# Splitting the last 256 tokens into two units of 128 and regrouping the opening in a two-layer transformer kernel

## The chip, the cores and the metric

The kernel runs on one NeuronCore of one Trainium2 chip. The metric is the device time of one execution in microseconds (us). Six runs of the kernel before gave a median of 1552.33 us, from 1551.97 to 1553.21.

The core has five engines with separate instruction streams, each executed in order. The text calls them PE (matrix multiply), ACT (activation functions), DVE (vector), POOL (GpSimd) and SP (here it only issues DMAs). PE writes its results into PSUM, eight banks of 128 partitions x 512 fp32.

## The reference: what is computed

2048 tokens of width 512 pass through attention, MLP, attention, MLP. Both attention layers share one set of weights, and so do both MLPs.

```python
def _A_ref(x, wqkv, wo):                       # D = 512, H = 32 heads of 16
    qkv = (x @ wqkv).reshape(B, S, 3, H, Dh).transpose(2, 0, 3, 1, 4)
    p = softmax(einsum("bhqd,bhkd->bhqk", q, k) * Dh ** -0.5)
    return einsum("bhqk,bhkd->bhqd", p, v).transpose(0, 2, 1, 3).reshape(B, S, D) @ wo
def _B_ref(x, w1, b1, w2, b2):                 # F = 1376
    return gelu(layernorm(x) @ w1 + b1) @ w2 + b2
x = x + _A_ref(layernorm(x), A_wqkv, A_wo)
x = x + _B_ref(layernorm(x), B_w1, B_b1, B_w2, B_b2)
x = x + _A_ref(layernorm(x), A_wqkv, A_wo)
x = x + _B_ref(layernorm(x), B_w1, B_b1, B_w2, B_b2)
```

A head has only 16 channels, so most of the work is not the multiplication but the exponentials: 2 layers x 32 heads x 2048 x 2048 of them.

## The kernel before

**Tiles.** Tokens lie in 16 tiles of 128. Query tokens are handled in units: four units of four tiles in layer 1 (the code's L == 1), and in layer 3 (the second attention) three units of four tiles and two of two tiles, tokens 12-13 and 14-15 (`build_segments`). Heads go in eight groups of four. A segment is one unit and one head group. The first unit of each layer is done in two parts over the keys (layer 1: key tiles 0 to 3 first, then 4 to 15), since its keys aren't all ready.

**A score tile** fills one PSUM bank with 512 columns: a unit of four tiles has 512 query columns for one key tile and one head; a unit of two tiles has two key tiles of 256 columns each, as two matmuls. There are 4096 score tiles in all. The four heads of a group lie in four row groups of PE (32 rows each), so up to four score tiles run side by side (L1470). The products with V (PV, L1658) use four column groups in the same way and accumulate in one bank (`ACCB`, 6).

**Exponentials.** ACT takes score tiles in groups: one instruction (L1455) reads two or three adjacent banks and writes bf16 probabilities. DVE takes about a quarter of the tiles in another way ("D tiles"): it adds a constant to the score, stores 16-bit integers whose bits are a bf16 approximation of the exponential (L1555), and adds shifts to make three more (L1588); each of the four is multiplied with a scaled V and accumulated. So a D tile costs PE four PV turns and an ACT tile one.

**Banks.** A pool "mb" owns banks 0 to 5 and 7. In the opening (layer 1, unit 0, part 0) scores use banks 0 to 3 in groups of two and two (`flow_scores`), and banks 4, 5 and 7 are left for other matmuls. Then `wide` is set: banks 0 to 5 belong to scores, in groups of three and two, and D tiles use bank 5 or 7.

**The opening.** While ACT does the scores of key tiles 0 to 3, the keys and values of tiles 4 to 15 are made (`job_qkv_tile` with "kv"): normalise into `xn` (L891, L893), transpose by a DMA that SP issues into `xnT` (L927), eight matmuls (L950) into a bank of mb, copies by DVE (L956, L973), squares by POOL (L991), norms by DVE (L1015). When the norms of all 16 tiles are there, `job_scl` makes one bound per head (L1157 to L1166), which scales the queries of every later segment (L1196). So part 1 can't begin before the last key tile is done.

**The end of a segment** (`job_segend`): DVE transposes the accumulated bank (L1688), takes a reciprocal (L1714) and writes the scaled output to `ob` (L1723). When eight head groups are done, `job_post` issues four transposing DMAs into `OT` (L1732), multiplies with wo (L1737), adds the residual, normalises, transposes (L1784), and `job_ffn` does w1 (L1792), bias (L1816), GELU on ACT (L1827, L1828, with one table load before and one behind, as exp and GELU lie in different tables), w2 (L1835) and the sum (L1837).

**The end of the kernel** (`job_tail`, `tail_tile`): for tokens 14-15 the residual and the first seven head groups are put into a bank ahead of the last one (L1898, L1737); after the last scores a GELU of one column loads the table (L1869); the last head group is added (L1903), the bank normalised straight from PSUM (L1907 to L1914), transposed by PE (L1916, L1918); then w1, GELU with the bias from PSUM (L1889) and w2 (L1874) follow chunk by chunk, 11 chunks of 128 hidden channels, and the result is copied out (L1879).

**The order of the work** is made at build time. `Sched` holds tasks with priorities and modelled durations, and always places next the one that can start first; its choices become the five in-order streams. `Hint.ORDER` is a string of digits: every four score groups it picks one of ten settings of the planner's thresholds (such as how idle DVE must be to take a D tile). Another string gives another order of the whole program. A last pass (`refill`) fills modelled PE gaps with matmuls on zeros (L1359, L1361, L1363), which keep PE busy and change no result.

Of the kernel before, what the change touches and what calls it, by code (L numbers as in the profile page):

```python
# [506 lines left out]

class Hint:
# [3 lines left out]
    ORDER = '1000505400844554053031008034310130004043277211200001031009349005902383344374250110710071520000700010897013450230200545450055021090000330009921105703053220050405100500340302221091514024010003201130050000322000100000400300044000720830007030033701430000245354444034510580430030403022240093200204095050982000792049091440853'  # L512
# [13 lines left out]
class Builder:  # L526
# [16 lines left out]
    def build_segments(self):  # L543
        self.segs = []
        four = [tuple(range(4 * c, 4 * c + 4)) for c in range(self.NC)]
        self.units = {1: four, 3: four[:3] + [four[3][:2], four[3][2:]]}
# [369 lines left out]
    def job_qkv_tile(self, L, tt, slot, i, left, prio, what):  # L916
# [10 lines left out]
        yield self.dma(lambda e: e.dma_start_transpose(xnT, xnr), [RX], [RXT], prio, 1.31, 1.2)  # L927
# [443 lines left out]
    def flow_scores(self):  # L1371
# [11 lines left out]
        for b in range(4):  # L1383
            S_.retire("mb", b, ("ret", b))
        last = {}
        while True:
# [6 lines left out]
            if not self.wide and not (sg["L"] == 1 and sg["nparts"] == 2 and sg["part"] == 0):  # L1393
                self.wide = True
                gi += gi % 2
                for b in (4, 5):
                    S_.retire("mb", b, ("ret", b))
            if self.wide:
# [49 lines left out]
            if len(ops[0]) > 1:  # L1448
                ops = [[o[i] for o in ops] for i in range(len(ops[0]))]
# [231 lines left out]
    def job_segend(self, sg):  # L1681
# [33 lines left out]
        if L == 3 and qc == len(self.units[3]) - 1 and hg == 7:  # L1715
            ob = self.obl[:, :].rearrange("p (b r) -> p b r", r=32)
            yield Task("dve", 1.2, [I(lambda e: e.tensor_tensor(out=ob[:, :, 0:16], in0=T[:, :, 0:16], in1=rv.unsqueeze(2).broadcast_to([128, nb, 16]), op=ALU.mult), [RA, ("rv", a)], [("obl",)], 0.147 + 0.268 * W / 512)])
# [22 lines left out]
    def post_prio(self, L, qc):  # L1740

        return 0.95 if L == 1 and qc >= self.NC - 2 else 2.2
# [45 lines left out]
    def mm_w1(self, L, qc, fc, b, pr, W, off=0):  # L1788
        M = 128 if fc < self.NFC - 1 else self.FLAST
        yield ("keys", [("w1", L, qc, fc)])  # L1790
        for c0 in (0, 2):
            yield Task("pe", pr if c0 == 0 else min(pr, HINT.LIN2), [I(lambda e, c=c: e.matmul(self.ps[0:M, b, off:off + W], lhsT=self.w1(fc, c), rhs=self.yT[:, c, 0:W], start=(c == 0), stop=(c == 3)),  # L1792
                                    [("wf", fc)] + [("yT", i) for i in range(W // 128)], [("ps", b)], 0.216 * W / 512, [("ps", b)]) for c in (c0, c0 + 1)])

    def gt(self, fc, i, W):
        if fc == self.NFC - 1:
            return self.g10[:, i * 128:(i + 1) * 128]
        return self.gv[:, fc * W + i * 128:fc * W + (i + 1) * 128]
# [220 lines left out]
```

## Time and profile before

| | before |
|---|---|
| median of six runs | 1552.33 us |
| the profiled execution | 1552.41 us, its span 1550.4 us, granted PE clock 1.000 |
| PE, DVE, ACT busy | 97%, 95%, 98% of the span |
| exponentials on ACT | 687 of two tiles, 586 of three |
| first exponential starts, first one behind the opening starts, last one ends | 20.95, 87.10, 1529.56 us |
| matmuls | 16485 |

The span runs from the first to the last instruction; the 2.0 us between it and the time lie around it. "Busy" is the union of an engine's instructions. Matmuls are pipelined, so one of 128 columns is shown with 219 ns though the next starts 56 ns later: start times tell more than durations. In a row of the timeline the first number is the start, the second the length of the merged row; what stands in brackets is idle time of that engine ahead of the row, and what ended it.

### The profile page before, as it was taken

The page shows a single profiled execution, that of the slowest core. Times are in us where ns is not written, and L with a number is a line of the kernel's source. Part 1 is how long each engine was busy: PE and PEld are TensorE (multiplying, and loading weights), DVE is VectorE, ACT ScalarE, POOL GpSimd, SP SyncE. Part 2 cuts the span into 40 slices and gives each one's busy share as a digit, 9 for nine tenths or more (in the row PEclk, how much of TensorE's full clock was granted, in tenths as well). Part 3 has the DMA queues.
Part 4 walks back from the last instruction along what each step waited for, and adds up shares of the span by engine and source line. Part 5 has one row for each costly group of instructions (what it writes and reads, how often), then busy time and mean ns, then how long its engine had stood idle before and what let it go on. Part 6 is the DMA issues. An engine that isn't in the chain of part 4 may idle for free.

```text
span 1550.4 us, 39363 instructions
## 1 busy us (share of the span) xinstructions
PE 1505.2 (97%) x16485; PEld 475.0 (31%) x16485; DVE 1465.3 (95%) x3272; ACT 1512.3 (98%) x1361; POOL 321.7 (21%) x558
## 2 busy tenths in 40 slices
PE   9999999999999999999999999999999999999998
PEld 3222222222222222222222322223222222344444
DVE  8799999999999999999999899999999999999993
ACT  8989999999999999999999999999999999999996
POOL 3585322002220021102312227310001000020100
PEclk9999999999999999999999999999999999999999
DMA  6673012214311222214732232310102000221200
GB/s 163 123 143 99 29 32 40 56 22 89 76 42 51 45 65 70 56 28 95 142 70 60 59 81 69 63 25 22 33 21 42 22 18 23 41 42 36 51 20 22
DMA packets 212450, 88.68 MB, mean 57 GB/s; under 512 B 183307, under 2 KB 207152, under 8 KB 212272
## 3 DMA queue, kind: packets, MB, share of 16 engines
q1 hardware_dynamic: 212272, 86.16, 25.3%
q8 instruction: 129, 2.11, 0.6%
q14 instruction: 49, 0.40, 0.1%
HBM read 34.65 MB, written 19.48 MB: 35 GB/s over the span
## 4 chain that ended last, share of the span: by engine, by line
ACT 47%; DVE 27%; PE 22%; issue 2%; POOL 1%; DMA 0%; SPq 0%; POOLq 0%; DVEq 0%
ACT PT L1455 44%; DVE dp L1555 11%; DVE dp L1588 8%; PE ps L1470 7%; PE ps L1658 5%; ACT h L1827 2%; PE ps L1835 2%; PE ps L1792 2%; PE ps L950 2%; PE ps L1359 1%; DVE accT L1688 1%; DVE n L1015 1%; DVE st L873 1%; PE ps L1068 1%; PE ps L1363 1%
## 5 line engine op out<-in xcount | busy, mean ns | idle before, releaser
L1455 ACT ACTIVATE PT<-ps 128x1536 bf16<-128x1536 f32 (+1 forms) x1273 | 1428.5, 1289 | 18.8 <-PE ps L1470 16.5
L1555 DVE TENSOR_SCALAR dp<-ps 128x512 uint16<-128x512 f32 x964 | 642.1, 681 | 27.3 <-PE ps L1470 25.6
L1470 PE MATMUL ps<-QT,KT 32*128 32x512 bf16 (+1 forms) x4608 | 600.9, 359 | 19.2 <-ACT PT L1455 6.0
L1588 DVE TENSOR_SCALAR dp<-dp 128x1024 uint16<-128x1024 uint16 (+1 forms) x1464 | 567.9, 429 | 3.6 <-PE ps L1658 0.9
L1658 PE MATMUL ps<-PT,V 128*17 128x512 bf16 (+1 forms) x3518 | 487.4, 358 | 0.1
L1658 PE MATMUL ps<-dp,vs 128*17 128x512 bf16 (+1 forms) x3270 | 464.0, 356 | 0.8 <-DVE dp L1588 0.6
L1470 PEld LDWEIGHTS ps<-QT,KT 32*128 32x128 bf16 x4608 | 161.9, 91 | 551.4 <-ACT PT L1455 302.9
L1196 POOL TENSOR_SCALAR QT<-qraw,scl,qbias 128x512 bf16<-128x512 bf16 (+1 forms) x83 | 72.8, 877 | 771.6 <-PE ps L1470 767.5
L1658 PE MATMUL ps<-dp,V 128*17 128x512 bf16 (+1 forms) x1090 | 224.1, 357 | 1.1 <-DVE accT L1688 0.6
L1363 PE MATMUL ps<-zw 128*32 128x448 bf16 (+16 forms) x1679 | 163.6, 325 | 0.9 <-DVE dp L1555 0.7
L1658 PEld LDWEIGHTS ps<-dp,vs 128*17 128x17 bf16 x3270 | 119.4, 88 | 122.9 <-issue 92.7
L1658 PEld LDWEIGHTS ps<-PT,V 128*17 128x17 bf16 x3518 | 117.5, 88 | 86.8 <-issue 72.8
L1361 PE MATMUL ps<-zw 32*128 32x444 bf16 (+4 forms) x443 | 131.7, 320 | 0.0
L1359 PE MATMUL ps<-zw 128*128 128x448 bf16 (+20 forms) x428 | 103.4, 340 | 4.4 <-DVE onec L754 2.1
L1792 PE MATMUL ps<-yT,wf 128*128 128x512 bf16 (+3 forms) x396 | 101.1, 359 | 2.2 <-DVE yT L1918 0.5
L950 PE MATMUL ps<-wqkv,xnT 128*128 128x512 bf16 x336 | 93.7, 382 | 4.8 <-DMA xnT<-xn 1.7
L1221 POOL TENSOR_SCALAR vs<-V 128x340 bf16<-128x340 bf16 (+2 forms) x72 | 62.9, 874 | 23.4 <-PE ps L1658 14.7
L1658 PEld LDWEIGHTS ps<-dp,V 128*17 128x17 bf16 x1090 | 54.6, 88 | 40.7 <-issue 25.8
L1363 PEld LDWEIGHTS ps<-zw 128*32 128x32 bf16 x1679 | 57.2, 95 | 25.6 <-DVE dp L1555 5.5
L1816 DVE TENSOR_SCALAR h<-ps,b1c 128x512 bf16<-128x512 f32 (+2 forms) x88 | 62.1, 705 | 2.3 <-PE ps L1792 2.2
L1688 DVE STREAM_TRANSPOSE accT<-ps 128x512 f32<-128x512 f32 (+1 forms) x88 | 57.9, 658 | 4.1 <-PE ps L1658 3.8
L1359 PEld LDWEIGHTS ps<-zw 128*128 128x128 bf16 x428 | 34.1, 99 | 61.4 <-issue 36.8
(182 smaller groups left out, 886.0 us busy)
## 6 DMA issues: line engine op xcount, KB each, us to landing
vs<-vs_scr SPq DMA_DIRECT2D x56, 255.0 KB, 2.8
wf<-in_B_w_dram SPq DMA_DIRECT2D x90, 128.0 KB, 2.9
q_scr<-qk SPq DMA_DIRECT2D x20, 256.0 KB, 2.3
k_scr<-qk SPq DMA_DIRECT2D x12, 256.0 KB, 2.0
out_dram<-xres SPq DMA_DIRECT2D x16, 128.0 KB, 1.7
vs_scr<-vs SPq DMA_DIRECT2D x8, 255.0 KB, 3.1
xres<-in_A_x_dram SPq DMA_DIRECT2D x7, 256.0 KB, 3.5
v_scr<-vst SPq DMA_DIRECT2D x12, 136.0 KB, 1.7
```

The costliest lines, as they stand in the source:

```text
L950: yield Task("pe", prio if c0 == 0 else min(prio, HINT.LIN2), [I(lambda e, c=c: e.matmul(self.ps[:, b, :], lhsT=xnT[:, c, :], rhs=self.wqk ...
L1196: yield Task(eng, 0.4, [I(lambda e: e.tensor_scalar(out=self.QT[:, q, 0:W], in0=src, scalar1=self.scl[:, k, hg:hg + 1], scalar2=self.qbias ...
L1359: fn = lambda e: e.matmul(self.ps[:, b, 0:w], lhsT=self.zw[:, 0:128], rhs=self.zw[:, 0:w], start=st, stop=st, skip_group_check=True)
L1361: fn = lambda e: e.matmul(self.ps[:, b, 0:w], lhsT=self.zw[32 * p:32 * p + 32, 0:128], rhs=self.zw[32 * p:32 * p + 32, 0:w], start=st, sto ...
L1363: fn = lambda e: e.matmul(self.ps[32 * p:32 * p + 32, b, 0:w], lhsT=self.zw[:, 0:32], rhs=self.zw[:, 0:w], start=st, stop=st, skip_group_c ...
L1455: S_.submit(Task("act", 1e-5 * gi, [I(lambda e, pt=pt, n=n, b0=b0: e.activation(out=self.PT[:, pt:pt + n, :], in_=self.ps[:, b0:b0 + n, :] ...
L1470: return [I(lambda e, kb=kb, i=i: e.matmul(self.ps[:, b, i * W:(i + 1) * W], lhsT=self.KT[32 * hp:32 * hp + 32, hg, kb * 128:(kb + 1) * 12 ...
L1555: self.S_.submit(Task("dve", 0.0, [I(lambda e: e.tensor_scalar(out=self.dp[:, u, w * 512:(w + 1) * 512], in0=self.ps[:, b, :], scalar1=BIT ...
L1588: yield Task("dve", pr, [I(lambda e, k=k, v=v: e.tensor_scalar(out=self.dp[:, v, 0:N], in0=self.dp[:, u, 0:N], scalar1=float(SHIFT[k]), sc ...
L1658: ops.append((nth[j, sh] + 0.1 * i, I(lambda e, hp=hp, v=v, ap=ap[:, i * W:(i + 1) * W], first=first and i == 0, W=W: e.matmul(self.ps[32 ...
L1688: yield Task("dve", 0.3, [I(lambda e: e.transpose(self.accT[:, a, 0:W], self.ps[:, ACCB, 0:W]), [("ps", ACCB)], [RA], 0.17 + 0.535 * W / 5 ...
L1792: yield Task("pe", pr if c0 == 0 else min(pr, HINT.LIN2), [I(lambda e, c=c: e.matmul(self.ps[0:M, b, off:off + W], lhsT=self.w1(fc, c), rh ...
```

## The change

- **Units.** The last two tiles become two units of one tile: `[12, 13], [14], [15]`. A score tile of such a unit is four key tiles of 128 query columns, four matmuls of 128 columns. The tail (`job_tail`) now handles tile 15 alone.
- **The held feed-forward.** Tile 14 goes through `job_post` and `job_ffn`, but its GELU waits for the key "warm", which the tail sets after the last scores, so it needs no table load of its own; its w2 follows in the tail. The tail's buffers move aside (`yT` columns 128 on, `gv` from 2048). The tail's OT transposes wait for "ffn1" (w1 issued) of the unit ahead instead of "post".
- **The last copy** of tile 15 is split in two halves, DVE and ACT.
- **The opening** uses groups of three and two on banks 0 to 4 (`OPEN5`); banks 5 and 7 are left for other matmuls. Score matmuls of groups are interleaved also where their lengths differ.
- **Four tiles** (4 to 7) are transposed by PE into a bank of mb and copied by DVE (`TPE`), instead of by DMA.
- `post_prio` gives units 3 and on of layer 3 the priority 0.95, and `Hint.ORDER` is another string.

```diff
+LATE3 = 3
+TPE = range(4, 8)
+OPEN5 = True
 class Hint:
-    ORDER = '10005054008445540530...'
+    ORDER = '10303145040130007700...'
...
-        self.units = {1: four, 3: four[:3] + [four[3][:2], four[3][2:]]}
+        self.units = {1: four, 3: four[:3] + [four[3][:2], four[3][2:3], four[3][3:]]}
...
-        yield self.dma(lambda e: e.dma_start_transpose(xnT, xnr), [RX], [RXT], prio, 1.31, 1.2)
+        if L == 1 and what == "kv" and tt in TPE:
+            b = yield ("get", "mb")
+            yield Task("pe", prio, [I(lambda e, k=k, b=b: e.transpose(self.psbf(b)[:, k * 128:(k + 1) * 128], xnr[:, k * 128:(k + 1) * 128], self.ident[:, :]), ...) for k in range(4)])
+            yield Task("dve", prio, [I(lambda e, b=b: e.tensor_copy(out=xnT, in_=self.psbf(b)[:, 0:512].rearrange("p (c t) -> p c t", c=4)), ...)])
+            S_.release("mb", b)
+        else:
+            yield self.dma(lambda e: e.dma_start_transpose(xnT, xnr), [RX], [RXT], prio, 1.31, 1.2)
...
-        for b in range(4):
+        for b in range(5 if OPEN5 else 4):
             S_.retire("mb", b, ("ret", b))
...
-                gi += gi % 2
-                for b in (4, 5):
+                if not OPEN5:
+                    gi += gi % 2
+                for b in (5,) if OPEN5 else (4, 5):
                     S_.retire("mb", b, ("ret", b))
-            if self.wide:
+            if self.wide or OPEN5:
                 b0, G = ((0, 3), (3, 2))[gi % 2]
...
-        return 0.95 if L == 1 and qc >= self.NC - 2 else 2.2
+        return 0.95 if L == 1 and qc >= self.NC - 2 or L == 3 and qc >= LATE3 else 2.2
...
-        if self.cur + 1 < len(self.segs):
+        last = L == 3 and qc == len(self.units[3]) - 2
+        if last:
+            yield ("keys", [("warm",)])
+        elif self.cur + 1 < len(self.segs):
...
-        yield ("keys", [("post",) + self.prev(L, qc)] + [("ot", L, qc, hg) for hg in range(7)])
+        yield ("keys", [("ffn1",) + self.prev(L, qc)] + [("ot", L, qc, hg) for hg in range(7)])
...
         yield Task("act", pr, [I(lambda e: e.activation(out=self.kmx[:, 2:3], in_=self.kmx[:, 0:1], func=ACTF.Gelu_apprx_tanh), ...)])
+        S_.mark(("warm",))
...
+                    for k, eng in enumerate(("dve", "act")):
+                        dst, src = self.xres[:, tt, 256 * k:256 * k + 256], self.ps[:, acc[i], 256 * k:256 * k + 256]
```

## The prediction

> **What bounds the kernel now.** First the page's busy times, then the chain that ended last, the ACT groups by shape, ACT's timeline in the opening and at the end, PE's timeline beside it, and the chain of the last 20 us.
>
> ```profile
> PE 1505.2 (97%) x16485; PEld 475.0 (31%) x16485; DVE 1465.3 (95%) x3272; ACT 1512.3 (98%) x1361; POOL 321.7 (21%) x558
> ACT 47%; DVE 27%; PE 22%; issue 2%; POOL 1%; DMA 0%; SPq 0%; POOLq 0%; DVEq 0%
> L1455 ACT ACTIVATE PT<-ps 128x1536 bf16<-128x1536 f32 x586 | 890.4, 1520 | 14.1 <-PE ps L1470 12.7
> L1455 ACT ACTIVATE PT<-ps 128x1024 bf16<-128x1024 f32 x687 | 737.9, 1093 | 4.7 <-PE ps L1470 3.8
> ```
>
> Three engines are nearly full and the chain passes among them, but ACT's exponentials are the pace. Their mean durations overlap; start to start, an undisturbed one of two tiles takes 0.905 us and one of three 1.330 (28 of two in 25.97 us below: 27 steps and a last one of 1.09 give 0.92 with the few short waits). Times these, 687 and 586 are 621.7 + 779.4 = 1401.1 us of the 1508.6 between first start and last end; eight GELU blocks and small work take most of the rest, and waits about 42.5.
>
> ```profile
> 20.95 25.97 ACT L1455 ACTIVATE PT<-ps 128x1024 bf16<-128x1024 f32 x28
> ...
> 82.25 1.94 ACT L1455 ACTIVATE PT<-ps 128x1024 bf16<-128x1024 f32 x2 [0.21 <-PE ps L1470]
> 87.10 3.71 ACT L1455 ACTIVATE PT<-ps 128x1536 bf16<-128x1536 f32 x3 [2.92 <-PE ps L1470]
> 1519.07 10.49 ACT L1455 ACTIVATE PT<-ps 128x1536 bf16<-128x1536 f32 x9
> ```
>
> The opening's 64 groups of two run from 20.95 to 84.18; ACT then stands still for 2.92 us, the longest wait in the body.
>
> ```profile
> 76.12 0.61 PE L950 MATMUL ps<-wqkv,xnT 128*128 128x512 bf16 x2
> 76.66 0.39 PE L1470 MATMUL ps<-QT,KT 32*128 32x512 bf16 x2
> 76.98 0.61 PE L1658 MATMUL ps<-PT,V 128*17 128x512 bf16 x8
> 80.85 1.04 PE L950 MATMUL ps<-wqkv,xnT 128*128 128x512 bf16 x4
> 85.65 0.17 PE L1165 MATMUL ps<-krhs,sel 32*128 32x8 bf16 x1
> 86.67 0.82 PE L1470 MATMUL ps<-QT,KT 32*128 32x512 bf16 x6
> ```
>
> Here PE makes the last key tiles between score pairs. The starts give its prices: two key matmuls 0.54 us (76.12 to 76.66), four 0.97, a score pair 0.32, eight PV matmuls 0.54. So a turn of 512 columns costs 0.2155 and each change of kind 0.107. After the last key matmul (81.9) the bound per head and the scaled queries take until 86.67, and nothing is left to fill them.
>
> ```profile
> 1530.00 0.32 PE ps L1898
> 1531.76 0.24 PE ps L1903
> 1532.03 1.30 DVE st L1907 x2
> 1534.71 1.54 DVE xn L1914 x2
> 1537.21 1.48 PE ps L1792 x12
> 1547.28 0.60 ACT xres L1879
> ```
>
> Behind the last exponential (1529.56) comes a chain of 20.84 us, of which the last feed-forward is 1537.21 to 1547.26.
>
> **The change part by part.** The sum is made against the profiled execution, 1552.41 us (span 1550.4 + 2.0 around it), 0.08 above the median.
>
> *Opening, -5.0.* The instruction lists of the two built programs say what PE issues. From the third key tile's matmuls to the last's, before: 71 changes of kind x 0.107 = 7.6, key matmuls 17.2, score turns 7.5, PV 4.7, together 37.1 us; the trace took 38.4 (43.4 to 81.9), so PE sets that stage, while ACT's 74 tiles there ask 37 x 0.905 = 33.5. After: 68 x 0.107 = 7.3, key matmuls with the 16 PE transposes 17.5, scores 6.9, PV 5.4: 37.0. But the score tiles that stand in that stretch are now 80, and in groups of three and two: 16 x (1.330 + 0.905) = 35.8. The two engines meet. And 13 tiles of scores (5.8 us) lie behind the last key matmul, where before 4 did, so the 4.8 us to the first wide scores are covered: the gap of 2.92 goes. Next late would be a score bank on PE's turn, of which I leave 3.9 us in the opening (5.3 before, in many steps of 0.2). 128 tiles cost 26 x 1.330 + 25 x 0.905 = 57.2 instead of 64 x 0.905 = 57.9. Together 2.92 + 0.7 + 1.4 = 5.0. Bounds: -6.1, where the waits halve; 0, where the two banks 5 and 7 (three before) hold up the key tiles. The transposes' other costs: 16 x 0.056 us on PE is in the 17.5; four copies of 0.41 on DVE lie where DVE has slack (in 80 to 100 us its sum is 18.7 of 20, with waits on ACT's side); four SP issues of 1.2 us go, and SP's queue loses them ahead of the later xnT. These are hidden by PE's own pace; without that cover four copies cost 1.6 us.
>
> *Fewer, larger groups in the body, -2.2.* The lists have 653 groups of two and 607 of three. Without the opening: before 623 x 0.905 + 586 x 1.330 = 1343.2, after 628 x 0.905 + 581 x 1.330 = 1341.0: five tiles go from ACT to DVE. Table loads and GELUs ahead of the last scores stay the same in number.
>
> *The last 256 tokens on PE, +0.5.* Priced in the same way, the last 256 score tiles cost PE 86.2 us before (256-column turns of 0.1095) and 87.3 after (128-column turns of 0.056). ACT asks 80 groups, 87.3, and one GELU block of 5.3 (1.28 + 2.34 + 0.42 + 1.28): 92.6. So PE has 5.3 us of slack. The narrow price rests on this row, whose eight full matmuls of 128 columns, each with its own weights, take 0.62 us: the last lasts 0.23, so the starts are 56 ns apart.
>
> ```profile
> 18.04 0.62 PE L1138 MATMUL ps<-ident,dp 128*128 128x128 bf16 x8
> 1450.00:1500.00 50.00, 48.91 (x849) 22.37 (x848) 46.06 (x110) 50.00 (x47) 5.42 (x10) 1.00 0.16 41
> ```
>
> The second row is busy time by engine (sum; PE, its loads, DVE, ACT, POOL; clock 1.00): in the units of 256 PE is full by that view, but zero fills are part of it. No row shows a long run of narrow turns in row groups. From below 56 ns (0, since the slack is not used in the sum); from above, the mean length of a load of 32x128, 92 ns in this stretch: some 760 narrow turns x 36 ns - 5.3 = +22. I take +0.5, near the row of the same width, with loads between.
>
> The Trainium skill speaks against it. Its page "TensorE: Matmul & The Clock Gate", section "Back-to-back issue gap", gives about 81 ns for each pair of load and matmul at 128 columns in a sustained stream, and 56 only for single pairs. By it the sum would have 760 x 25 ns - 5.3 = an estimated +14 in place of +0.5, and the time would be about 1559. The eight pairs of the row above stand at 56 ns, though eight are a short stream.
>
> *DVE in the last units, +1.0.* 16 segment ends of one tile (each about 0.55, 8.8) for 8 of two (0.69, 5.6): +3.2. The held tile's bias additions, 11 x 0.25 = 2.8, its norm and residual about 1.8, five more D tiles x 1.13 = 5.6. That is 13 us, in a kernel where DVE idles 85; but in the last 92 us DVE's sum comes to about 92. The work that hides it is ACT's exponentials of the same stretch. Bounds 0 (spread over earlier idle time) and +3.2 (the segment ends all late). I take +1.
>
> *SP, 0.* Sixteen query transposes of 128 for eight of 256 (1.1 us to issue), four more OT transposes (1.25), eight more loads: about 40 of the last 92 us, in a queue that has room. Uncovered, an OT transpose costs its 1.25 + 2.4 to land; that is in the tail.
>
> *Tail, -1.3.* One tile instead of two: statistics 1.30 to 0.65, normalising 1.54 to 0.77, transposes and copy -0.46, POOL -0.3, w1 and w2 10.05 to 44 x 0.056 + 11 x 0.2155 + 0.5 = 5.4, last copy -0.2: -7.0. Against it: the tail now issues, behind the last scores, the held tile's 44 w1 matmuls (2.5), its GELU of 1280 (1.3 after the table load, from 4.47 at 5120 and 2.34 at 2560), then 11 w2 matmuls (2.4), and the o-projection of the first seven head groups only behind these, on OT transposes that go out after head group 6's `ob`: 4 x 1.25 + 2.4 - so the last head group's product ends at about 6.6 us behind the last exponential, and the statistics start at 7.5 rather than 2.47: +5.0, and 0.7 as a margin towards the upper bound. Bounds -2.9 (the transposes go earlier) and +1.5 (they and w2 add up).
>
> *Another planner string, 0.* It reorders the whole program. Waits in the body were 33 us before; the lists show the same bursts per tile. Bounds -4 and +6, the spread of 50 us stretches (0.6 to 4 us each) over ten of them.
>
> Sum: -5.0 - 2.2 + 0.5 + 1.0 - 1.3 + 0 = -7.0, so 1545.4 us.
>
> **The rivals.** *R1, the opening does not gain.* Of the two banks 5 and 7 for key tiles one is at times held by a PE transpose until its copy: if production slips by 5 us, part 1 still starts near 87. For it: PE is the pace there already. Against: 13 tiles of cover. Time 1550.4.
>
> *R2, the other side: narrow matmuls run at their loads' pace.* Place: the scores of tiles 14 and 15, four matmuls of 128 columns where two of 256 stood. Price 0.76 us for each ns above 56. Slack gone at 63 ns, all gain at about 73, and from there slower; at 88 to 92 ns +20, 1565. For it: loads here last 92. Against: the row at 56.
>
> *R3, the new order waits more elsewhere*: +6 over the body, 1551.4. For it: in 650 to 1100 us the old order already lost 17. Against: nothing says the new one is worse.
>
> *R4, the tail is later*: the o-projection behind w2 costs 3 more, 1548.4. That the change does nothing is excluded: the lists differ in every engine.
>
> **How the numbers follow.** Chances: forecast 0.56 (1541.5 to 1548), R1 0.14 (1548 to 1552), R2 0.10 (1555 to 1566), R3 0.12 (1548 to 1556), R4 0.08 (1547 to 1550). A difference under 0.2% (3.1 us) is about what a measurement can't tell from none. Faster means under 1549.2: the forecast, most of R4, a third of R1 and a quarter of R3: 0.70. Slower means over 1555.4: R2 and a little of R3: 0.12. Within: 0.18. The range from 1541 to 1554 leaves out R2 and the ends of others.
>
> **What would show it.** Opening right: the first wide exponential at about 82, no gap over 1 us ahead of it; wrong: still near 87, with L965 waiting for banks. Narrow turns right: score bursts of 128 columns with starts 56 ns apart and ACT's steps of 0.905 and 1.330 kept in the last 92 us; wrong: waits of ACT on PE there of more than 6 us together. Tail right: span end about 19.5 us behind the last exponential, statistics at about +7.5. Order: waits of ACT over 100 to 1440 us near 30. What would make the whole wrong is a pace of narrow turns above 73 ns.

## The result, and the profile after

The changed kernel is slower: 1556.39 us median of 17 runs (1553.81 to 1560.11) against 1552.44 of 38 runs of the kernel before; the ratio is 1.0024 with a 95% interval of 1.0018 to 1.0031. The forecast was 1545.4, with 1541 to 1554 as its range. One execution of the run open_tuned below took 4254 us and is left out of its ratio.

The first profile caught the slowest execution, 1560.11 us. A second one, of the same kernel (the run after_again below), is 1555.60 us, its span 1553.8: it is close to the median, and the comparisons below use it where nothing else is said. First the page's busy times and its chain by engine, then ACT's groups by shape, all from the first profile.

```profile
PE 1500.5 (96%) x17698; PEld 492.1 (32%) x17698; DVE 1478.0 (95%) x3319; ACT 1513.0 (97%) x1350; POOL 321.4 (21%) x569
ACT 35%; DVE 31%; PE 29%; POOL 2%; issue 2%; DMA 1%; SPq 0%; POOLq 0%; DVEq 0%
```

```profile
L1470 ACT ACTIVATE PT<-ps 128x1536 bf16<-128x1536 f32 x607 | 916.9, 1511 | 18.0 <-PE ps L1485 16.1
L1470 ACT ACTIVATE PT<-ps 128x1024 bf16<-128x1024 f32 x653 | 703.3, 1085 | 6.5 <-PE ps L1485 5.6
```

The exponentials are as few as forecast, 653 x 0.905 + 607 x 1.330 = 1398.3 us. But ACT stands still for 24.5 us ahead of them (18.8 before), and the chain runs through DVE and PE for 60% of the span (49% before): ACT sets the pace less often.

ACT's timeline of the opening, from after_again, answers to the lines of the opening before.

```profile
20.93 11.65 ACT L1470 ACTIVATE PT<-ps 128x1536 bf16<-128x1536 f32 x10
...
52.87 22.92 ACT L1470 ACTIVATE PT<-ps 128x1536 bf16<-128x1536 f32 x20 [0.22 <-PE ps L1485]
75.99 6.14 ACT L1470 ACTIVATE PT<-ps 128x1536 bf16<-128x1536 f32 x5 [0.19 <-PE ps L1485]
82.39 5.54 ACT L1470 ACTIVATE PT<-ps 128x1024 bf16<-128x1024 f32 x5 [0.26 <-PE ps L1485]
```

Tile 128, the last of the opening, is done at 82.1, and part 1 follows without a gap at 82.39; before, it began at 87.10. So ACT gains 4.7 us there (4.0 in the first profile, where part 1 begins at 83.07), near the 5.0 forecast, and the question is where they went.

The table follows them. A "score tile" is done when its exponential ends, on ACT or as a D tile's load on DVE; ends are counted in order of time. ACT's waits are the start-to-start times of its exponentials less 0.905 and 1.330, without the GELU blocks, good to some 0.5 us. Tiles that one instruction makes are done together, so a row of the table can be off by a microsecond.

| score tile | done, before | after_again | first profile | ACT's waits since the row above, before / after_again |
|---|---|---|---|---|
| 128 | 84.2 | 82.1 | 82.8 | 8.3 / 4.3 |
| 256 | 137.7 | 134.3 | 134.9 | 3.1 / 4.5 |
| 512 | 224.6 | 222.5 | 223.2 | 1.4 / 3.6 |
| 1280 | 497.4 | 495.4 | 496.8 | 4.6 / 4.4 |
| 2688 | 1024.3 | 1023.3 | 1025.3 | 18.6 / 21.3 |
| 3840 | 1427.7 | 1426.6 | 1428.7 | 5.7 / 7.0 |
| 4096, the last exponential | 1529.6 | 1532.4 | 1536.9 | 1.0 / 5.1 |
| end of the span | 1550.4 | 1553.8 | 1558.3 | |

Three things stand in it. The opening's gain of 4.7 has shrunk to some 3.5 by tile 256, to 2.1 by tile 512, and to 1.1 (or to a loss of 1.0) by tile 3840. The last 256 tiles take 105.8 us instead of 101.8, in the first profile 108.2. The end behind the last exponential takes 21.4 us instead of 20.8.

From the last 256 tiles of the first profile: PE's timeline, ACT's, and windows (time; busy time of PE, its loads, DVE, ACT and POOL; granted clock; DMA's share and GB/s).

```profile
1464.68 0.29 PE L1485 MATMUL ps<-QT,KT 32*128 32x128 bf16 x6
1466.91 0.29 PE L1485 MATMUL ps<-QT,KT 32*128 32x128 bf16 x6 [1.94 <-issue]
...
1469.41 0.60 PE L1673 MATMUL ps<-dp,V 128*17 128x128 bf16 x16
```

```profile
1467.24 3.42 ACT L1470 ACTIVATE PT<-ps 128x1536 bf16<-128x1536 f32 x3 [1.70 <-PE ps L1485]
```

```profile
1464.00:1468.00 4.00, 2.06 (x68) 1.02 (x58) 1.79 (x4) 2.30 (x3) 0.45 (x1) 1.00 0.39 100
1468.00:1472.00 4.00, 3.88 (x121) 2.67 (x118) 3.60 (x8) 3.61 (x4) 0.00 (x0) 0.60 0.11 37
1469.00:1472.00 3.00, 3.00 (x98) 2.19 (x94) 2.70 (x7) 2.61 (x3) 0.00 (x0) 0.50 0.13 44
```

In the middle of a burst of twelve score matmuls PE stops for 1.94 us and nothing that the profile shows holds it ("issue"). ACT then waits 1.70 us. From 1468.8 the granted clock is 0.50 for 3.4 us (0.60 in the mean of the window of 4 us), and sixteen PV matmuls take 0.60 us that elsewhere take 0.40. A second such stretch begins at 1526.8, behind a wait of PE for DVE of 1.24 us.

### The profile page after: what moved, and what is told of

It is laid out like the page before. It is cut to its first block, busy times and chain, and to the rows that moved or that the text cites. A ratio compares the mean times of both kernels' runs of the same rounds, so it can differ in the third digit from the quotient of the medians.

```text
span 1558.3 us, 41905 instructions
## 1 busy us (share of the span) xinstructions
PE 1500.5 (96%) x17698; PEld 492.1 (32%) x17698; DVE 1478.0 (95%) x3319; ACT 1513.0 (97%) x1350; POOL 321.4 (21%) x569
## 4 chain that ended last, share of the span: by engine, by line
ACT 35%; DVE 31%; PE 29%; POOL 2%; issue 2%; DMA 1%; SPq 0%; POOLq 0%; DVEq 0%
ACT PT L1470 34%; DVE dp L1570 12%; DVE dp L1603 9%; PE ps L1485 9%; PE ps L1673 8%; PE ps L1854 3%; PE ps L1807 3%; PE ps L965 2%; PE ps L1374 1%; DVE accT L1703 1%; DVE st L882 1%; DVE n L1030 1%; PE ps L1378 1%; ACT h L1846 1%; DVE h L1831 1%
## 5 line engine op out<-in xcount | busy, mean ns | idle before, releaser
L1470 ACT ACTIVATE PT<-ps 128x1536 bf16<-128x1536 f32 (+1 forms) x1260 | 1429.6, 1290 | 24.5 <-PE ps L1485 21.7
L1485 PE MATMUL ps<-QT,KT 32*128 32x512 bf16 (+2 forms) x5120 | 602.6, 340 | 26.9 <-DVE dp L1570 9.9
L1673 PE MATMUL ps<-PT,V 128*17 128x512 bf16 (+2 forms) x3899 | 479.1, 339 | 0.5 <-issue 0.5
L1673 PE MATMUL ps<-dp,vs 128*17 128x512 bf16 (+2 forms) x3663 | 456.6, 338 | 1.0 <-DVE dp L1603 0.8
L1211 POOL TENSOR_SCALAR QT<-qraw,scl,qbias 128x512 bf16<-128x512 bf16 (+2 forms) x91 | 71.5, 786 | 797.7 <-PE ps L1485 793.8
L1673 PE MATMUL ps<-dp,V 128*17 128x512 bf16 (+2 forms) x1221 | 221.2, 338 | 3.3 <-DVE accT L1703 3.0
L1378 PE MATMUL ps<-zw 128*32 128x448 bf16 (+20 forms) x1491 | 153.0, 323 | 1.1 <-DVE dp L1570 0.9
L1376 PE MATMUL ps<-zw 32*128 32x444 bf16 (+5 forms) x392 | 120.9, 331 | 0.0
L1807 PE MATMUL ps<-yT,wf 128*128 128x512 bf16 (+5 forms) x440 | 101.9, 340 | 4.7 <-DVE dp L1603 2.1
L1374 PE MATMUL ps<-zw 128*128 128x448 bf16 (+16 forms) x409 | 100.3, 341 | 4.7 <-DVE onec L763 2.1
L1831 DVE TENSOR_SCALAR h<-ps,b1c 128x512 bf16<-128x512 f32 (+3 forms) x99 | 65.6, 667 | 3.8 <-PE ps L1807 3.2
```

The source lines that it names most:

```text
L1374: fn = lambda e: e.matmul(self.ps[:, b, 0:w], lhsT=self.zw[:, 0:128], rhs=self.zw[:, 0:w], start=st, stop=st, skip_group_check=True)
L1376: fn = lambda e: e.matmul(self.ps[:, b, 0:w], lhsT=self.zw[32 * p:32 * p + 32, 0:128], rhs=self.zw[32 * p:32 * p + 32, 0:w], start=st, sto ...
L1378: fn = lambda e: e.matmul(self.ps[32 * p:32 * p + 32, b, 0:w], lhsT=self.zw[:, 0:32], rhs=self.zw[:, 0:w], start=st, stop=st, skip_group_c ...
L1470: S_.submit(Task("act", 1e-5 * gi, [I(lambda e, pt=pt, n=n, b0=b0: e.activation(out=self.PT[:, pt:pt + n, :], in_=self.ps[:, b0:b0 + n, :] ...
L1485: return [I(lambda e, kb=kb, i=i: e.matmul(self.ps[:, b, i * W:(i + 1) * W], lhsT=self.KT[32 * hp:32 * hp + 32, hg, kb * 128:(kb + 1) * 12 ...
L1673: ops.append((nth[j, sh] + 0.1 * i, I(lambda e, hp=hp, v=v, ap=ap[:, i * W:(i + 1) * W], first=first and i == 0, W=W: e.matmul(self.ps[32 ...
```

## The experiments

Each run stands beside runs of the kernel before on the same chip. Medians are in us; the ratio is against the kernel before, with its 95% interval.

### The changed kernel again

No edit.

> The changed kernel again, unaltered. Its first profile (1560.11 us) has PE idle for 1.94 us at 1464.97 with nothing to wait for, just behind the load of a block of its instructions, and a granted clock of 0.60 in the 4 us after 1468. Theory A (PE runs out of instructions in the dense last units, and the idle time lowers the clock): an execution nearer 1554 shows the same instruction blocks loaded every 4 us, but no PE gap over 0.6 us and no clock under 0.95 before the last exponential; ACT's waits on PE behind 1440 us are then about 4 us instead of 7.4. Theory B (the end is slow by the order of its work): waits of 7 us there at any clock, and the difference between executions lies elsewhere. Median 1555 to 1557 by both.

Measured: 1555.60, ratio 1.0020 (1.0011 to 1.0029). PE's waits from 1440 to 1533 us:

```profile
PE ps L1485 <- issue: 2.2, 2, 1.5
PE ps L1485 <- DVE dp L1570: 1.2, 1, 1.2
PE ps L1673 <- issue: 0.9, 1, 0.9
```

The pauses without a releaser are there again, 3.1 us in three, the longest 1.49 us and between the same two groups of score matmuls. The clock stays at 1.00. So theory A is half wrong: the pauses belong to the kernel and not to its longer executions, and a pause does not always bring the clock down. The clock does go with the spread. Of the first 18 executions of the changed kernel the six at a granted clock of 1.000 took 1553.8 to 1555.5, the seven at 0.998 or less 1556.6 to 1560.1; of the eleven of after_again the three at 1.000 took 1555.0 to 1555.6, the three at 0.998 or less 1556.0 to 1558.7. But the clock is not the whole loss: the kernel before, at 1.000, has medians of 1552.1 to 1552.7 on the different chips.

### The opening alone

The two parts of the change that concern the opening (`OPEN5`, `TPE`) are put into the kernel before, with the new string.

```diff
+TPE = range(4, 8)
+OPEN5 = True
-    ORDER = '10005054008445540530...'
+    ORDER = '10303145040130007700...'
```

> The kernel before with the opening of the change (groups of three and two, four tiles turned by PE) and the new planner string; the last 256 tokens and the tail as before. The order of every engine is that of the changed kernel up to about 1400 us. Theory C (the opening gains some 4 us and the body under the new order gives them back before 640 us): the time that score tile 3840 is done is 1 us later than before, the whole 1552 to 1554. Theory D (the opening's gain lasts, all that was lost is lost in the last 256 tokens and the tail): 1547 to 1549.

Measured: 1555.92, ratio 1.0020 (1.0011 to 1.0029). Tile 256 is 2.6 us early and tile 3840 0.9 late: the gain is given back in the body, as theory C has it, though the median lies above its range. The last 256 tiles take 104.6 us; that the string's last digits were made for other units is the likely cause. The next run chooses them anew:

```diff
-    ORDER = '...'            # digits 282 on: for units of 128
+    ORDER = '...'            # digits 282 on: for the two units of 256
```

> The opening of the change with the last 256 tokens and the tail of before, as in the run open_new, but with the string's digits behind place 282 chosen anew for this ending (in open_new they belonged to the units of 128, and the last 256 score tiles cost 2.3 us more than in the kernel before). Up to about 1350 us every engine's order is that of the changed kernel. Theory C (of the 5 us that the opening gains, 4 are given back in the body): tile 256 is done 4 to 5 us earlier than before, tile 3840 between 1.5 earlier and 1 later, the whole 1551 to 1553.5. Theory D (the opening's gain lasts): 1547 to 1549.

Measured: 1553.58, ratio 0.9997 (0.9988 to 1.0006). The opening alone is worth nothing that the medians show; at a granted clock of 1.000 the five executions have a median of 1552.0, those of the kernel before 1552.4. The profile, of an execution of 1554.77 us, has tile 128 2.1 us early, tile 256 only 1.4 (theory C said 4 to 5), tile 512 on time and tile 3840 1.4 late. Part of that is the clock, in open_tuned and, with the same order up to there, in after_again:

```profile
91.00:96.00 5.00, 5.00 (x27) 1.00 (x27) 4.12 (x7) 2.97 (x3) 3.16 (x5) 0.50 0.95 220
```

```profile
91.00:96.00 5.00, 4.67 (x37) 1.34 (x36) 5.00 (x11) 4.48 (x4) 4.10 (x8) 1.00 0.97 216
```

So what the opening is worth at tile 512 is read from after_again, 2.1 us.

### The string alone

```diff
-    ORDER = '10005054008445540530...'
+    ORDER = '10303145040130007700...'
```

> The kernel before with the new planner string and nothing else. Theory G (a string fits only the structure that it was made for): more than 10 us slower, spread over the whole body as short waits of ACT and fewer D tiles. Theory H (strings are shuffles of equal worth): 1549 to 1556.

Measured: 1600.32, ratio 1.0302 (1.0284 to 1.0321). The page's busy times, and ACT's waits, here and in the kernel before:

```profile
PE 1526.1 (95%) x16698; PEld 492.4 (31%) x16828; DVE 1460.3 (91%) x3229; ACT 1530.8 (96%) x1368; POOL 325.4 (20%) x558
```

```profile
ACT PT L1455 <- PE ps L1470: 39.4, 81, 3.3
```

```profile
ACT PT L1455 <- PE ps L1470: 16.5, 37, 2.9
```

Theory G: 48 us. ACT waits 81 times instead of 37, and has 1280 exponentials instead of 1273, as 16 D tiles fewer are taken. So this string is no shuffle among equals: it fits the structure that it was made for. It could not be judged apart from the opening, and "Another planner string, 0", with bounds of -4 and +6, stood for a choice that can be worth tens of microseconds.

### Where DVE's work costs

Ten instructions are put into DVE's finished stream, once between 140 and 215 us and once between 30 and 75.

```diff
+        at = [i for i, op in enumerate(prog.streams["dve"]) if LO <= op.t0 <= HI and any(r[0] == "ps" for r in op.reads)]
...
+                if i in at:            # ten of these places
+                    e.bn_stats(out=junk[:, k, :], in_=zw[:, :])
```

> The kernel before, its order unchanged, with ten more DVE instructions (statistics of 448 constant columns into a place that nobody reads, by the row of the same operation some 0.6 us each, 6 us in all) put between its own from 140 to 215 us. Theory I (DVE is the limit there: it isn't idle for a microsecond from 137 to 223 us): score tile 512 is done 4 to 6 us later and the whole is 1555.5 to 1558.5. Rival (DVE is full there only since it takes D tiles when it has room): order is fixed, so waits of PE on DVE's banks show, but under 2 us: 1553 to 1555.

> The same ten DVE instructions between 30 and 75 us, in the opening, where DVE is idle 20 us in all. Theory I: score tile 128 is done at most 1 us later and the whole stays within 1552 to 1554. Rival (the key tiles' chain through DVE is what makes the opening long): tile 128 comes 3 to 6 us later.

Measured: 1558.39, ratio 1.0033 (1.0020 to 1.0046), and 1552.14, ratio 0.9998 (0.9989 to 1.0007). The ten take 6.1 us of DVE in both (0.61 each). In the body tile 512 comes 6.0 us later, microsecond for microsecond; in the opening tile 128 comes 0.4 later. Windows of the kernel before, 30 to 80 and 140 to 220 us:

```profile
30.00:80.00 50.00, 49.23 (x329) 13.24 (x327) 36.29 (x72) 47.60 (x51) 24.57 (x41) 1.00 0.70 126
140.00:220.00 80.00, 77.13 (x917) 22.63 (x913) 79.81 (x180) 79.26 (x75) 28.37 (x44) 1.00 0.13 37
```

DVE is the third number: 36.3 of 50 us in the opening, 79.8 of 80 in the body. The same windows of after_again:

```profile
30.00:80.00 50.00, 49.41 (x363) 14.64 (x360) 42.43 (x86) 48.03 (x43) 26.17 (x43) 1.00 0.65 131
140.00:220.00 80.00, 76.69 (x897) 22.94 (x893) 79.97 (x180) 78.92 (x75) 28.88 (x49) 1.00 0.15 39
```

Up to tile 512 DVE's books come out. Its busy time (union) until then is 203.1 us before and 207.2 after, its idle time 21.5 and 15.3. The new opening saves 6.2 us of DVE's idle time and DVE has 4.1 us more to do, of which four PSUM copies are 1.6 and the D tiles' shifts 2.8 (133 for 130, 0.475 us each for 0.465). What is left is 2.1, which is what tile 512 is early by. From tile 256 to 512 DVE has 2 to 3 us more work in the changed kernel, mostly norms and scalings of query tiles which before were done by then. PE waits for DVE soon after part 1 has begun; in after_again:

```profile
87.91 0.60 PE L1485 MATMUL ps<-QT,KT 32*128 32x512 bf16 x4 [0.91 <-DVE dp L1570]
```

The kernel before has no such wait there.

The converse takes DVE's work away between 95 and 215 us, in the kernel before and in that of the run open_tuned:

```diff
-                ins = op.fn(eng)
+                ins = op.fn(eng, N=64) if i in cut else op.fn(eng)     # 20 of the shifts of 1024 columns
```

> The kernel before, order unchanged, with 20 of the DVE shifts (1024 columns, 0.456 us each) between 95 and 215 us done on 64 columns only, which takes some 6 us of work from DVE there; the rest of those probabilities stays what it was, so the attention is not the reference's. ACT's waits from tile 128 to 512 are 4.5 us, so at most that can be won. Theory I (DVE sets the pace there): tile 512 is done 2 to 4 us earlier, the whole 1549 to 1551. Rival J (ACT and PE are as full): under 1 us, 1552.

> The same cut in the kernel of the run open_tuned (opening of the change, ending of before; 1553.6 us, ACT's waits from tile 128 to 512 are 9.8 us in its profile). Theory I: what the opening won comes back once DVE is eased: tile 512 5 to 7 us earlier than in open_tuned, the whole 1547 to 1549, that is 2 to 4 us under before_relief where open_tuned stood 1 over before. Theory K (the new order loses it whatever DVE has to do): within 1 us of before_relief or over it.

Measured: 1550.40, ratio 0.9984 (0.9976 to 0.9993), and 1548.86, ratio 0.9970 (0.9959 to 0.9982). Each cut shift takes 0.21 us, so 4.9 us go. In the profiles tile 512 comes at 223.4 and 219.0, where the kernel before has 224.6 and the new opening 222.5 (after_again; open_tuned's 224.6 holds the low clock). So the same cut is worth 1.2 us to tile 512 with the old opening and 3.5 with the new one: with DVE eased, the opening's lead at tile 512 is 4.4 us instead of 2.1, nearly all of its 4.7. That bears theory I out for the new opening. In the kernel before its 2 to 4 us at tile 512 were not reached, so there ACT and PE are nearly as full as DVE, as rival J has it. At the end the lead is 1.5 us by the medians, where the forecast said 2 to 4; the profile loses some of it from tile 1664 to 2176, where ACT waits 7.9 us instead of 5.9.

A last pair eases DVE without leaving anything out:

```diff
+            if getattr(op.fn, "move", False) and LO <= op.t0 <= HI:     # the scaling into ob
+                spec = ("pool",) + spec[1:5] + (0.75, 0.38)
```

> The kernel before, order unchanged, but the scaling of a segment's output into ob (128x512 with the reciprocal, 0.43 us on DVE) is done by POOL for the 61 segments that end between 90 and 1390 us: 26 us of work off DVE, spread over the body. ACT's waits there are about 33 us. Theory I (DVE's load makes these waits): 1548 to 1551. Rival (the order is fixed to DVE's old load, and POOL beside DVE slows its shifts): 1552 to 1554.

> The same move in the kernel of the run open_tuned (opening of the change, ending of before). Theory I: the opening's gain shows again: 2 to 4 us under ob_pool, 1546 to 1549. Theory K (the new order loses it whatever DVE has to do): within 1 us of ob_pool.

Measured: 1552.62, ratio 1.0001 (0.9992 to 1.0010), and 1552.30, ratio 0.9999 (0.9990 to 1.0008). Both are misses by the medians, though the two executions of open_ob_pool at a granted clock of 1.000 took 1549.3 and 1549.8, too few to settle it. ACT's waits from tile 128 to 512 stay at 4.4 and 9.2 us; the second profile has the low clock from 90 us again. DVE's groups by shape say in part why, from 100 to 1390 us; its shifts in the kernel before and in ob_pool:

```profile
L1588 DVE TENSOR_SCALAR dp<-dp 128x1024 uint16<-128x1024 uint16 x1284 | 502.7, 433 | 3.3 <-PE ps L1658 0.9
```

```profile
L1591 DVE TENSOR_SCALAR dp<-dp 128x1024 uint16<-128x1024 uint16 x1285 | 511.3, 441 | 3.6 <-PE ps L1661 1.2
```

DVE is rid of 24 us (56 scalings of 0.428), but its shifts cost 8.6 us more while POOL works, and the stretch that counts had only some seven of the scalings. By its median, nothing measured here beats the kernel before without leaving work out.

### The end alone

The changed kernel with the opening and the string of before.

```diff
-TPE = range(4, 8)
+TPE = ()
-OPEN5 = True
+OPEN5 = False
```

> The changed kernel with the opening of before (groups of two and two, all tiles turned by DMA) and the old string, so two units of 128, the held feed-forward, the split last copy and the priority 0.95 alone. Up to about 1400 us every engine's order is that of before. Theory A: the end costs 3 us in an execution at full clock and up to 7 with gaps, 1555 to 1560, spread over more than 3 us. Theory E (the end is worth something and only the new string spoils it): 1550 to 1552. By the prediction's terms (+0.5 +1.0 -1.3) it would be 1552.6.

Measured: 1555.48, ratio 1.0018 (1.0009 to 1.0027). In its profile (1553.85 us, clock 1.000) the last 256 tiles take 106.1 us, 4.3 more than before, and the end behind the last exponential 19.1, 1.8 less. The end costs some 3 us by itself; with the opening it costs no more, as the opening gains nothing.

### Instructions or columns

Every score and PV matmul of the last two units is cut in two, in PE's finished stream of the kernel before:

```diff
+            def halves(run):           # a burst on different tiles, behind its waits
+                for op in run:
+                    op.fn(eng, 0, 128)
+                for op in run:
+                    ins = op.fn(eng, 128, 256)
```

> The kernel before, order and work unchanged, but each score and PV matmul of 256 columns in the last two units is issued as two of 128, so that PE has about 2600 more matmuls there for the same columns. Theory A (supply of instructions): the blocks of 256 instructions come at most every 3.6 us, PE gets gaps without a releaser and the clock dips; 1556 to 1562. Theory B: two turns of 56 ns for one of 109.5 cost 1.7 us of 86 on PE, hidden in its slack: 1552 to 1553.5. Theory F (narrow matmuls run at the pace of their loads, 90 ns): about 20 us more, 1570.

Measured: 1564.49, ratio 1.0075 (1.0062 to 1.0087), between the ranges of theories A and F. But the edit does more than it was meant to: the order is not unchanged. It collects matmuls into a burst as long as they lie on different tiles of PE and none of them waits, and a score's row tile and a PV's column tile count as different. So where PV follows the scores without a wait, the last scores and the first four PV matmuls are cut as one burst. One such place, in the kernel before and in split_half:

```profile
1473.21 0.39 PE L1470 MATMUL ps<-QT,KT 32*128 32x256 bf16 x6
1473.54 0.28 PE L1658 MATMUL ps<-dp,V 128*17 128x256 bf16 x1
...
1474.08 0.40 PE L1470 MATMUL ps<-QT,KT 32*128 32x256 bf16 x6
```

```profile
1483.85 0.34 PE L1489 MATMUL ps<-QT,KT 32*128 32x128 bf16 x9
1484.13 0.22 PE L1681 MATMUL ps<-dp,V 128*17 128x128 bf16 x1
...
1484.29 0.23 PE L1489 MATMUL ps<-QT,KT 32*128 32x128 bf16 x3
1484.45 0.23 PE L1681 MATMUL ps<-dp,V 128*17 128x128 bf16 x1
...
1484.95 0.40 PE L1489 MATMUL ps<-QT,KT 32*128 32x128 bf16 x11
```

Scores and PV took 0.87 us (1473.21 to 1474.08). Now nine scores, four PV matmuls, three scores and the rest of PV take 1.10 (1483.85 to 1484.95). From 1340 us on PE changes between scores and PV 310 times instead of 196. The 56 places with the two extra changes take 11.7 us more in all, 0.23 in the median; the 44 pairs of scores and PV without them take 0.3 less in all. The whole profile is 13.2 us longer. So nearly all of the loss is the changes of kind (114 at the prediction's 0.107 us are 12.2) and not the 2804 matmuls, which cost next to nothing where the order was kept. Pauses without a releaser are 1.2 us from 1340 to 1545 us:

```profile
PE ps L1681 <- issue: 1.2, 2, 0.8
```

So this run does not speak for theory A. Then only the score matmuls:

```diff
-                    f.__dict__["half"] = W == 256       # PV
+                    f.__dict__["half"] = False
```

> As the run split_half (1564.5 us for 2804 more matmuls), but only the 1024 score matmuls of the last two units are split in two, so that PE's instructions rise from some 43 to some 53 per us there. Theory A (a limit of about 256 instructions in 3.4 to 3.8 us, 67 to 75 per us): under it, so at most 1.5 us more: 1552 to 1554. Rival (each further matmul costs its share, 11.7 us x 1024 / 2804 = 4.3): 1556 to 1557.5.

Measured: 1553.19, ratio 1.0002 (0.9993 to 1.0011): within 1 us, where a share of the cost would be 4.3. PV stays whole here, so nothing is mixed (198 changes between scores and PV). A matmul more costs next to nothing here too, as theory A said and as split_half's theory B would have it; the rival's price rested on split_half's loss. What the supply of instructions looks like shows in the queue that loads PE's. Its row for 1470 to 1520 us (blocks, MB, share), in the kernel before, score_half, split_half and after_again:

```profile
q8 instruction: 7, 0.11, 0.9%
```

```profile
q8 instruction: 9, 0.15, 1.3%
```

```profile
q8 instruction: 12, 0.20, 1.6%
```

```profile
q8 instruction: 12, 0.20, 1.6%
```

A block is 16 KB, 256 instructions (a load of weights and a matmul are two): the 129 blocks of the kernel before hold 33024, and it has 32970 matmuls and loads. Twelve in 50 us are one in 4.2 us. By their start times the shortest interval from 1440 to 1532 us is 5.75 us before, 4.01 in score_half, and 3.38 in split_half and in after_again; the median is 7.2, 5.6, 3.8 and 4.2 us. None came faster than 3.38. Each pause without a releaser of 0.4 us or more, in after_again and in the first profile, ends 2.3 to 2.6 us behind the start of a block's load, so PE seems to wait for that block. At 56 ns for a turn of four column tiles a stretch of PV alone would use 256 instructions in 1.8 us. But the rate does not decide it: in the densest 20 us PE runs 67 instructions per us in after_again, 68 in end_alone and 70 in split_half, and the pauses from 1440 to 1533 us are 3.1, 0.1 and 0.5 us. What makes a block late in the one kernel and not in the other stays open.

The other direction takes instructions away from the changed kernel, at the same columns:

```diff
+                few = getattr(op.fn, "few", None)            # (which of the four key tiles, 4) in units of 128
+                if few and few[0] < few[1] - 1 and not op.sig:
+                    continue
+                ins = op.fn(eng, 0, 512) if few and few[0] == few[1] - 1 else op.fn(eng)
```

> The changed kernel, its order and its waits unchanged, but in the units of 128 the four score matmuls of a tile, and the four PV matmuls of a probability tile, are one of 512 columns (with the weights of the last of the four key tiles): the same columns for a quarter of the instructions. It leaves out the other key tiles, so attention of tokens 14 and 15 is not that of the reference. Theory A (PE is short of instructions there): no PE gap without a releaser over 0.4 us behind 1440 us, ACT's waits in the last 256 score tiles fall from 5.1 to between 1 and 2 us, executions lie closer together, and the median is 1551 to 1552.5. Rival B (the order of DVE's and PE's work in the last units costs it): 1555 to 1556.5 as before.

> The same cut to a quarter of the instructions, in the run end_alone (old opening, old string; 1555.5 us; it also leaves out three of four key tiles for tokens 14 and 15). Theory A: ACT's waits in the last 256 score tiles fall from 3.7 to 1 to 1.5 us, the whole is 1552 to 1553.5; what stays against the kernel before is the four D tiles that went to ACT (1.6 us) less the shorter tail (1.7). Rival B: 1555 to 1556.

Measured: 1552.10, ratio 0.9999 (0.9990 to 1.0008), and 1554.07, ratio 1.0013 (1.0004 to 1.0022). PE's waits of after_few from 1440 to 1533 us, to be held against those of after_again:

```profile
PE ps L1489 <- DVE dp L1577: 1.5, 2, 1.3
PE ps L1489 <- ACT PT L1473: 0.8, 4, 0.3
...
PE ps L1864 <- issue: 0.3, 2, 0.2
```

The pauses are down to 0.5 us (0.3 and a second row of 0.2), the last 256 tiles take 103.7 us instead of 105.8, and the median falls by 3.5 us, or by 3.0 when each run is held against the kernel before on its own chip. That is about what the pauses took. PE changes between scores and PV as often in both, 107 times from 1430 us on. So the number of PE's instructions, and not their columns, costs the changed kernel most of what it loses. In end_alone, which has no such pauses, it is 0.9 us of 2.6, each again against its own chip (ACT's waits 3.7 to 3.0, not to 1.5 as expected). The rest there is four D tiles fewer, hence four exponential tiles more on ACT (some 1.7 us), and short waits of ACT whose cause stays open. Whether DVE's work is what these tiles still cost in after_few was asked with DVE's shifts cut there too, by the edit of open_relief between 1405 and 1490 us:

> The run after_few (1552.1 us; a quarter of the instructions in the units of 128) with 20 DVE shifts of the last 256 score tiles done on 64 columns, some 6 us of DVE's work taken away; two parts of the computation are left out. Theory L (the 2.3 us that these tiles still cost there are DVE's, by its segment ends): ACT's waits in them fall from 2.8 to about 1, the whole is 1549.5 to 1551. Rival (they are PE's turns): 1552 as before.

Measured: 1552.67, ratio 0.9996 (0.9987 to 1.0005). In the profiles ACT's waits in these tiles fall from 2.8 to 1.1 us and the tiles take 102.0 us instead of 103.7; the medians show nothing. The profile speaks for DVE, the times don't confirm it.

## Why the prediction was wrong

Against the forecast after_again stands so. Opening and body: -7.2 forecast, -1.1 measured at tile 3840. The last 256 tiles: +1.5 forecast, +4.0 measured. The end behind them: -1.3 forecast, +0.6 measured. Together that is -7.0 and +3.5 (3.4 between the spans).

*The step that failed first* is the sum's handling of the opening: "the gap of 2.92 goes" and its other gains entered as 5.0 us of the whole, with "Another planner string, 0" behind them. Of the 5.0, 4.7 were there at the start of part 1 (4.0 in the first profile). Behind it DVE is full for some 120 us, and a lead of ACT is soon used up there. The prediction put the four copies "where DVE has slack", by a window that ends at 100 us, and counted DVE's idle 85 us over the whole span; 21 of them lie ahead of tile 256, and from there to tile 512 there is 0.2. The work that the shorter opening no longer covered came due in that stretch. That DVE takes the gain back there is shown by adding work (+6.0 us at tile 512) and by taking it away (a lead of 4.4 us at tile 512 instead of 2.1). What is lost behind tile 512, 1 to 2.5 us, differs from execution to execution, and its cause stays open. PE's waits for DVE's D tiles double from 85 to 1430 us. In the kernel before:

```profile
PE ps L1470 <- DVE dp L1555: 3.9, 15, 0.5
```

and in after_again:

```profile
PE ps L1485 <- DVE dp L1570: 8.0, 22, 0.9
```

*Fewer, larger groups, -2.2.* The exponentials are the 1398.3 us that the lists said. The five tiles that left ACT are five D tiles on DVE. The term was real, but between tile 128 and tile 3840 ACT's waits grew by some 6 to 7 us, of which about half lies ahead of tile 512; for the waits behind it no run shows the cause.

*The last 256 tokens on PE, +0.5.* Measured are 4.0 us in the last 256 tiles with DVE's part, of which 2.1 go with the instructions in the profile and 3.0 in the medians. The pace was nearly right: PV turns of 128 columns start 56 ns apart in the median, 60 in the mean, scores 67 to 75 in the median. At 63 ns the prediction saw the slack gone; by its own price a mean of some 65 ns over both kinds uses up PE's 5.3 us and costs little beyond. Its slack was set by an ACT that asks 92.6 us, with one GELU block; in both kernels these tiles hold a second one, of 7.7 us (1442.21 to 1449.95 before), so the size of the slack is not sure. What the sum had no term for are PE's pauses. It gave the matmuls' count (16485 to 17698) and priced columns and changes of kind only. The rival R2 had the right place and the wrong mechanism, the loads' length of 92 ns.

The Trainium skill's 81 ns for a sustained pair of load and matmul at 128 columns ("TensorE: Matmul & The Clock Gate", section "Back-to-back issue gap") do not fit the rows here: groups of four column tiles start 56 ns apart in the median, and so do 44 pairs on the whole array, w1 of the held tile in after_again:

```profile
1532.07 2.62 PE L1807 MATMUL ps<-yT,wf 128*128 128x128 bf16 x44
```

On the pauses its page "Runtime: NRT & Kernel Launch", section "Instruction fetch mechanics", says that instructions come in blocks of 16 KiB, 256 of them, as the runs show, and that their loading is hidden since instructions are issued more slowly than the blocks come. In these last units it seems not always hidden: pauses of 3.1 us in after_again, 0.5 in after_few.

*DVE in the last units, +1.0.* The 1.9 us that these tiles still cost in after_few's profile, and the 1.7 that few_relief's wins back, would put it near 2, inside its bounds; the medians don't confirm it.

*Tail, -1.3.* Measured +0.6, and -1.7 in end_alone. The last feed-forward was right: w1 and w2 take 5.4 us (1545.32 to 1550.76). Ahead of it the chain of after_again, behind its last exponential at 1532.41:

```profile
1532.07 1.29 PE ps L1807 x20
1533.40 0.36 DVE h L1831
...
1536.25 1.28 ACT h L1846
1537.55 0.32 ACT g L1847
1537.92 2.55 PE ps L1854 x11
1540.46 0.86 PE ps L1752 x4
1541.33 0.23 PE ps L1928
1541.58 0.71 DVE st L1932
```

The statistics start 9.2 us behind it, not 7.5. The held tile's w1 is issued so late that the eleven bias additions, 1533.40 to 1536.25, lie on the path in front of the GELU. The prediction had counted them as hidden work of DVE. In end_alone the same work stands earlier in the order, and the statistics start at 6.8:

```profile
1539.82 0.71 DVE st L1932
```

*The rivals.* R3, waits elsewhere, came nearest: it put 6 us on the body, and some 6 to 7 were measured. It named no cause but the order; up to tile 512 the cause is DVE. R1 did not happen: PE finished the key tiles at 75.6 us instead of 81.9, two banks were enough.

## What to carry to other kernels

Where several engines are nearly full, a gain at one place lasts only if the engine that bounds the next stretch gains too: take each engine's idle time stretch by stretch, and move a gain of one through it before it goes into the sum. Count the instructions and the changes of kind of an edit beside its columns, and look in the trace for pauses that nothing released. Check an experiment's edit in its trace before reading its time: one here cut the right matmuls and also changed their order, and the order was the whole cost. An order found for one structure is part of that structure: changed alone, it cost 48 us here.

## What the runs showed of the hardware

- PE's instructions came in blocks of 256, never closer than 3.38 us in the last units. PE paused there with nothing to wait for, up to 1.94 us, and such pauses ended 2.3 to 2.6 us behind the start of a block's load. The rate alone did not decide it: 67 per us over 20 us went with 3.1 us of pauses in after_again, 68 with 0.1 in end_alone, 70 with 0.5 in split_half.
- Two extra changes between scores and PV cost PE 0.23 us in the median of 56 places (split_half). Cutting matmuls of 256 columns into two of 128 cost nothing where the order was kept (44 pairs of scores and PV), and under 1 us for 1024 score matmuls.
- The granted clock fell to 0.50 for 3.4 us at a time. In the first profile this came 1.9 us behind a pause of PE of 1.94 us and 1.2 us behind a wait of 1.24; in after_few 0.9 us behind a wait of 1.28. It stayed at 1.00 behind a pause of 1.49 and a wait of 1.24 in after_again, and fell at 974.5 us in open_new with no pause of 0.9 us or more in the 45 us ahead. What makes it fall was not settled. A PV turn at 0.50 took 107 ns instead of 56.
- DVE's shifts of 1024 columns took 433 ns in the kernel before, and 441 with 24 us of its work on POOL.
